# A DRAM buffer of its own for the last piece of each group, and kk loads in two parts

## The chip, the cores and the metric

The kernel runs on one core of one Trainium2 chip. The metric is device time in microseconds, from one launch. Three runs of the kernel before are shown, and one further execution was recorded by the hardware profiler; all rows below come from that one.

## The reference

Three stages, all in float32, chained. Only the first matters for the change.

```python
# q, k, v, a_re, a_im: (batch 4, heads 8, steps 768, 48)
scale = np.minimum(mag, 0.999) / (mag + 1e-06)          # mag = |a|
a_re_n, a_im_n = (a_re * scale, a_im * scale)
for t in range(S):
    new_re = ar * S_re - ai * S_im
    new_im = ar * S_im + ai * S_re
    S_re, S_im = (new_re + k[t] outer v[t], new_im)      # state 48 x 48 per head
    y[:, :, t] = q[t] @ S_re
# then, on x = y as (3072, 384):
#   mixture of 8 experts, one expert per row: gate * (relu(x @ w1[e]) @ w2[e])
#   out = ((x @ w1) * (x @ w2)) @ w3 @ w_out
```

## The kernel before, in words

**The work of the first stage.** The 768 steps are cut into three *groups* (NG = 3) of 256, a group into four chunks of 64 steps (C = 64). Within a chunk the recurrence is rewritten as products: with P(t) the running product of the complex factors a, the kernel forms q(t) P(t) and k(t) divided by P(t), so that a chunk is an ordinary masked attention of 64 steps plus the state handed over from the chunk before.

**Pieces, the elementwise stream.** `elementwise` (line 722) works with 128 lanes; a lane is one (pair of batches q, chunk c, head h, batch b of the pair), so lanes 0 to 63 are q = 0 and lanes 64 to 127 are q = 1. It runs over 24 *pieces* of 8 steps (TP = 8), eight to a group (NPC = 8). For each piece it loads a (line 710, two pieces in one load) and the raw q and k (line 719), makes the scaled factors on ScalarE and VectorE, the running product step by step on VectorE (lines 780 and 782), and with line 812 the tile `qk` of that piece: 8 steps, two kinds (q P and k / P), 96 numbers. Some of its additions run on TensorE as matmuls with the identity (line 736). The piece is then stored to the DRAM tensor `qkd` (line 607), whose order is group, q, c, head, b, step, kind, 96. The seven first pieces of a group are stored by one DMA from GpSimd's queue (line 820); the last one is split, lanes 0 to 63 by SyncE (line 817) and lanes 64 to 127 by GpSimd (line 818).

**Tiles, the second stream.** `groups` (line 1026) takes the eight (q, c) *tiles* of each group in turn. For a tile, `loads` (line 898) issues on SyncE two loads of v into the buffer `vz` (line 907, six slots) and one load of `kk` (line 909, four buffers, 768 KB): 128 partitions (b, step), in each 8 heads x 2 kinds x 96 numbers. So the DRAM tensor does the transposition from lanes to steps. `turn` (line 885) transposes kk on TensorE (line 893) and copies the result to SBUF on ScalarE (line 894); then follow the scores (line 921), the state chain (lines 978, 985, 992 to 994), the outputs (lines 940, 941) and the routing to experts (lines 109 to 163). At the start of a group, `ends` (line 867) prepares the group's last factors; in the first two groups it also issues eight dense matmuls on the last stored piece (`dense`, line 879).

**What orders the work.** Both streams are generators that `drive` interleaves by costs written in the code, so that the first tile loads of a group are written behind the store of its eighth piece (line 1051 waits for `made` to reach the end of the group, line 1054 issues the loads of the group's first two tiles; those of later tiles are issued at line 1069, after a tile's chain). That gives every instruction its place in the program. The Tile framework then sorts the instructions of each engine's queue by this order and by a simulated time at which they become ready, adds the waits, and an engine executes its queue strictly in order; a load may so be issued long before its place in the program. Dependencies through DRAM are tracked by address ranges. In a lane of `qkd` the eight pieces lie behind one another, so the range of any tile's first seven pieces also spans parts of its eighth.

In the third group VectorE, ScalarE and SyncE also convert weights for the last stage (class `Fuse`; lines 282 to 297), which use SyncE's queue for the `fdr` loads. After the groups follow the experts (`moe`) and the last stage (`moe2`), both almost all TensorE matmuls.

Of the kernel before, what the change touches and what calls it, by code (L numbers as in the profile page):

```python
# [8 lines left out]
F32 = mybir.dt.float32  # L9
# [86 lines left out]
def bc(ap, n, at):  # L96
    shape = list(ap.shape)
    return ap.unsqueeze(at).to_broadcast(shape[:at] + [n] + shape[at:])
# [463 lines left out]
NH = 8  # L562
SEQ = 768
D = 48
C = 64
NG = 3
TP = 8
NPC = C // TP
NPIECE = NG * NPC
R2 = 2 * D  # L570
# [16 lines left out]
def attn_consts(tc, S):  # L587
    nc = tc.nc
    c = S.cpool
    S.mask = c.tile([128, C], F32, tag="mask", name="mask")  # L590
    nc.gpsimd.memset(S.mask, 1.0)
    for h in range(2):
        m = S.mask[h * C : (h + 1) * C, :]
        nc.gpsimd.affine_select(out=m, in_=m, compare_op=ALU.is_ge, fill=0.0, base=0, pattern=[[1, C]], channel_multiplier=-1)
    S.perm = c.tile([R2, R2], F32, tag="perm", name="perm")
    nc.gpsimd.memset(S.perm, 0.0)
    nc.gpsimd.affine_select(out=S.perm, in_=S.perm, compare_op=ALU.not_equal, fill=1.0, base=D, pattern=[[1, R2]], channel_multiplier=-1)
    nc.gpsimd.affine_select(out=S.perm, in_=S.perm, compare_op=ALU.not_equal, fill=-1.0, base=-D, pattern=[[1, R2]], channel_multiplier=-1)
    S.wb = c.tile([128, 1], F32, tag="wb", name="wb")
    nc.gpsimd.memset(S.wb, 0.4995)  # L600
    S.tiny = c.tile([128, 2], F32, tag="tiny", name="tiny")
    nc.gpsimd.memset(S.tiny[:, 0:1], 2.0 ** -60)
    nc.gpsimd.memset(S.tiny[:, 1:2], 2.0 ** -100)
    S.sy = c.tile([128, NPIECE], F32, tag="sy", name="sy")
    S.su = c.tile([128, NPIECE], F32, tag="su", name="su")
    S.xm = c.tile([128, NG, D], F32, tag="xm", name="xm")
    S.qkd = S.dpool.tile([NG, 2, 4, NH, 2, C, 2, R2], F32, tag="qkd", name="qkd")


class Fuse:  # L610
# [85 lines left out]
class Attn:  # L696
# [25 lines left out]
    def elementwise(self, aside, factors):  # L722

        nc, S, ep, e2 = self.nc, self.S, self.ep, self.e2
# [74 lines left out]
        def keys(i):  # L799
            g, p = divmod(i, NPC)  # L800
            k = raw[i][:, :, 1]
            x, g0 = s2[i][:, 0], s2[i][:, 1]
            if p == NPC - 1:
                v.tensor_copy(S.xm[:, g], px[i][:, E - D :])
            v.tensor_tensor(out=x, in0=px[i], in1=g0, op=ALU.mult)
            yield 470
            v.tensor_tensor(out=k, in0=k, in1=td(g0), op=ALU.mult)
            yield 470
            v.scalar_tensor_tensor(out=k, in0=td(x), scalar=2.0, in1=k, op0=ALU.subtract, op1=ALU.mult, reverse0=True)
            yield 470  # L810
            self.qk[i] = o = self.qp.tile([128, TP, 2, 2, D], F32, tag="qk", name=f"qk{i}")
            S.end = v.tensor_tensor(out=o, in0=bc(P[i], 2, 2), in1=bc(raw[i], 2, 3), op=ALU.mult)
            yield 1740
            dst = S.qkd[g].rearrange("q c h b (p t) w e -> p (q c h b) (t w e)", p=NPC)[p]
            self.stored = self.qk.pop(i).rearrange("p t w r d -> p (t w r d)")
            if p == NPC - 1:
                nc.sync.dma_start(dst[:64], self.stored[:64])
                done = nc.gpsimd.dma_start(dst[64:], self.stored[64:])
            else:
                done = nc.gpsimd.dma_start(dst, self.stored)  # L820
            with self.tc.issue_after(done.ins):
                aside(i)
            self.made = i + 1
# [21 lines left out]
        for i in range(NPIECE + 1):  # L845
            if i:
                power(i - 1)
                weigh(i - 1)
            if i % 2 and i + 3 < NPIECE:
                a[i + 3], a[i + 4] = self.load_a(i + 3)  # L850
            if i + AHEAD < NPIECE:
                root(i + AHEAD)
            if i + 1 < NPIECE:
                raw[i + 1] = self.load_qk(i + 1)
            ends = [j >= 0 and j % NPC == NPC - 1 for j in (i - 2, i - 1)]
            rest = [keys(i - 2)] if i > 1 and not ends[0] else []
            if i + 1 < NPIECE:
                rest.append(norm(i + 1))
            if ends[1]:
                rest.append(keys(i - 1))  # L860
            if i + 2 < NPIECE:
                rest.append(excess(i + 2))
            yield from mix(*([prefix(i)] if i < NPIECE else []), chain(*rest))
            if i == NPIECE - 1:
                factors()
# [30 lines left out]
        self.qkT[u] = qkT  # L896

    def loads(self, u):
        nc, S, st = self.nc, self.S, self.st
        g, q, c = u  # L900
        t0 = (g * 4 + c) * C
        n = self.nv
        self.nv = (n + 1) % VBUF
        assert n not in self.held.values()
        self.held[u] = n
        for i in range(2):
            nc.sync.dma_start(self.vz[i * C : (i + 1) * C, n, i], S.v[2 * q + i, t0 : t0 + C, :])
        kk = st.tile([128, NH, 2, R2], F32, tag="kk", name="kk%d%d%d" % u, bufs=4)
        nc.sync.dma_start(kk, S.qkd[g, q, c].rearrange("h b t w e -> (b t) h w e"))
        return self.vz[:, n].rearrange("t i (h e) -> t i h e", e=D), kk  # L910

    def scores(self, u, qk):
# [113 lines left out]
    def groups(self, route, side, free):  # L1026

        nc, S, st = self.nc, self.S, self.st
        self.ca, self.cb, self.cc, self.at, self.qkT, self.xs = {}, {}, {}, {}, {}, []
        self.route = route  # L1030
        self.nv = self.slot = 0
        self.held = {}
        self.pool, self.turns = [], 0
        self.spare = None
        self.vz = st.tile([128, VBUF, 2, HD], F32, tag="vz", name="vz")
        nc.gpsimd.memset(self.vz, 0.0)
        for q in range(2):
            self.ca[q] = st.tile([R2, 2, HD], F32, tag=f"ca{q}", name=f"ca{q}")
            self.cc[q] = st.tile([R2, 2, HD], F32, tag=f"cc{q}", name=f"cc{q}")
            nc.gpsimd.memset(self.ca[q], 0.0)  # L1040
        yield lambda: self.made >= NPC
        self.W = self.pp.tile([128, 2, 512], F32, tag="W", name="W")
        work = [(g, q, c) for g in range(NG) for q in range(2) for c in range(4)]
        ld = {}
        step = 0
        for n, u in enumerate(work):
            g, q, c = u
            if q == 0 and c == 0:
                while self.pool and self.made < (g + 1) * NPC:
                    yield self.fill(1)  # L1050
                yield lambda: self.made >= (g + 1) * NPC
                yield from self.ends(g)
                for x in work[n : n + 2]:
                    ld[x] = self.loads(x)
                if g == NG - 1:
                    yield free
                    singles, spare = side.fuse.units, side.product
                    side()
            self.pool.append(Item("scores", self.scores(u, ld[u][1])))
            for x in self.chain(u, ld.pop(u)):  # L1060
                yield x
                yield self.fill(S.fillcost)
                step += 1
                if g == NG - 1:
                    for _ in range(1 + (step % 3 == 0)):
                        next(singles, None)
            for x in work[n + 1 : n + 3]:
                if x[0] == g and x not in ld:
                    ld[x] = self.loads(x)
        self.spare = spare  # L1070
        while self.pool:
            yield self.fill(1)
# [146 lines left out]
def build(ctx, tc, S):  # L1219
# [4 lines left out]
    nc.scalar.preload_act_table_set("natural_log_exp_and_others")  # L1224
    make_consts(tc, S)
    attn_consts(tc, S)
    S.xbufs, S.fillcost = XB, FILL
    with ExitStack() as at:
# [99 lines left out]
```

## Time and profile before

| | us |
|---|---|
| median of 3 runs | 1030.84 (1028.14 to 1032.24) |
| profiled execution, its own time | 1032.15 |
| span of that execution, first to last instruction | 1030.5 |
| TensorE (PE) busy in the span | 904.5 (88%) |
| VectorE (DVE) busy | 635.0 (62%) |
| ScalarE (ACT) busy | 486.8 (47%) |

The profile names engines PE (TensorE matmul), PEld (its weight load), DVE, ACT, POOL (GpSimd) and SP (SyncE; SPq is its DMA queue). All times in its rows count from the span's start. The groups' eighth pieces are stored at about 108, 220 and 313 us; the second stream of the first stage ends at about 414 us. "idle before <- X" is the time an engine stood still and what ended it.

### The profile page before, as it was taken

Reading aid. Unit: us, or ns where it says so; the run is one execution under the profiler, and the core shown is the slowest. Engines: PE = TensorE matmul, PEld = TensorE weight load, DVE = VectorE, ACT = ScalarE, POOL = GpSimd, SP = SyncE. Lnnn points to the kernel's source line nnn. Section 1 sums busy time; section 2 is a strip of 40 time slices with the busy share of each in tenths; the row PEclk is TensorE's granted clock in tenths of the full one; section 3 lists DMA queues with packets and bytes.
Section 4 is the critical chain, followed back from the end, with each engine's and each line's share of the span. In section 5 each row is a group of like instructions: output and inputs, shape, how many; then the busy total and the mean of one; then the engine's idle time right before and its main releaser. Section 6 shows DMA issues by size and latency. Waiting matters only on the chain. (4 is left out here: it accounts for less than half of the span.)

```text
span 1030.5 us, 17151 instructions
## 1 busy us (share of the span) xinstructions
PE 904.5 (88%) x6402; PEld 768.3 (75%) x6402; DVE 635.0 (62%) x1398; ACT 486.8 (47%) x1089; POOL 124.4 (12%) x196
## 2 busy tenths in 40 slices
PE   3435899968987999879999899999999999999991
PEld 1212478737866778879999789997888888888881
DVE  6899899988986778878999555543132323232220
ACT  6445688848864655435666444443121312121220
POOL 5111000220011001000122120110010101010101
PEclk8666899989987989999999999999999999999996
DMA  5556975459548633646676564530000000000001
GB/s 184 174 175 224 311 250 169 141 161 321 165 152 257 185 120 114 214 159 193 192 199 175 138 159 108 108 57 0 1 31 1 31 1 31 1 31 1 31 1 35
DMA packets 90190, 128.82 MB, mean 125 GB/s; under 512 B 7232, under 2 KB 72688, under 8 KB 90096
## 3 DMA queue, kind: packets, MB, share of 16 engines
q1 hardware_dynamic: 79408, 87.26, 29.4%
q0 software_dynamic: 10688, 40.36, 11.1%
q8 instruction: 53, 0.87, 0.4%
q14 instruction: 41, 0.34, 0.1%
HBM read 92.38 MB, written 35.22 MB: 124 GB/s over the span
## 5 line engine op out<-in xcount | busy, mean ns | idle before, releaser
L547 DVE TENSOR_TENSOR ab<-asb,pb 128x512 f32<-128x512 f32 x48 | 33.0, 688 | 189.6 <-PE pb L303 183.6
L297 DVE TENSOR_TENSOR l<-w,h 128x384 fp32r<-128x384 f32 x128 | 70.7, 556 | 50.3 <-ACT h L296 47.1
L296 ACT CAST h<-w 128x384 fp32r<-128x384 f32 x128 | 65.2, 513 | 76.8 <-PE ph L302 39.2
L542 ACT COPY asb<-pa 128x512 f32<-128x512 f32 x48 | 28.1, 586 | 123.4 <-PE pa L303 123.4
L736 PE MATMUL x<-s,ident 128*128 128x384 f32 x64 | 35.3, 691 | 50.9 <-ACT s L788 50.9
L296 ACT CAST gh<-ab 128x512 fp32r<-128x512 f32 x48 | 29.8, 621 | 94.3 <-DVE ab L547 94.3
L301 PE MATMUL py<-hh,h 128*128 128x432 f32 x192 | 69.5, 362 | 2.9 <-ACT hh L357 2.9
L302 PE MATMUL py<-hl,h 128*128 128x432 f32 x192 | 70.3, 366 | 1.1 <-DVE hl L358 1.1
L301 PE MATMUL ph<-xh,h 128*128 128x432 f32 x192 | 68.9, 361 | 1.0 <-DVE hl L358 1.0
L303 PE MATMUL ph<-xh,l 128*128 128x432 f32 x192 | 69.1, 360 | 0.0
L302 PE MATMUL ph<-xl,h 128*128 128x432 f32 x192 | 69.0, 359 | 0.0
L303 PE MATMUL py<-hh,l 128*128 128x432 f32 x192 | 68.9, 359 | 0.0
L780 DVE TENSOR_TENSOR pr<-cf,P 128x192 f32<-128x192 f32 x189 | 66.8, 354 | 3.2
L893 PE MATMUL tr<-ident,kk 128*96 128x128 f32 x384 | 58.7, 289 | 9.4 <-DMA kk<-qkd 8.0
L302 PE MATMUL po<-ol,gh 128*128 128x384 f32 x192 | 64.9, 338 | 0.0
L301 PE MATMUL po<-oh,gh 128*128 128x384 f32 x192 | 64.9, 338 | 0.0
L303 PE MATMUL po<-oh,gl 128*128 128x384 f32 x192 | 63.4, 338 | 0.0
L736 PEld LDWEIGHTS x<-s,ident 128*128 128x128 f32 x64 | 15.0, 257 | 64.5 <-ACT s L788 56.8
L894 ACT COPY qkT<-tr 96x512 f32<-96x512 f32 x96 | 53.7, 591 | 17.2 <-PE tr L893 16.8
L514 POOL DMA_INDIRECT out<-ob,mdp x24 | 23.8, 992 | 308.9 <-ACT ob L511 217.1
L301 PE MATMUL pa<-yh,ah 128*128 128x512 f32 x144 | 57.2, 397 | 2.0 <-ACT yh L296 2.0
L893 PEld LDWEIGHTS tr<-ident,kk 128*96 128x96 f32 x384 | 43.0, 133 | 19.7 <-DMA kk<-qkd 9.6
(221 smaller groups left out, 2438.4 us busy)
## 6 DMA issues: line engine op xcount, KB each, us to landing
w<-in_w SPq DMA_DIRECT2D x128, 192.0 KB, 3.2
kk<-qkd SPq DMA_DIRECT2D x24, 768.0 KB, 6.7
qkd<-qk POOLq DMA_DIRECT2D x21, 768.0 KB, 5.5
qkr<-in_qk SPq DMA_DIRECT2D x24, 384.0 KB, 3.8
a<-in_a SPq DMA_DIRECT2D x11, 768.0 KB
fdr<-in_w SPq DMA_DIRECT2D x16, 512.0 KB, 5.1
fdr<-in_v POOLq DMA_DIRECT2D x12, 512.0 KB, 4.8
xs<-zr POOLq DMA_DIRECT2D x8, 648.0 KB, 7.3
```

Source lines behind the costliest of these rows:

```text
L296: nc.scalar.copy(H, src)
L297: nc.vector.tensor_tensor(out=L, in0=src, in1=H.bitcast(F32), op=ALU.subtract)
L301: nc.tensor.matmul(out, lh, rh, start=first, stop=False)
L302: nc.tensor.matmul(out, lh, rl, start=False, stop=False)
L303: return nc.tensor.matmul(out, ll, rh, start=False, stop=last)
L514: nc.gpsimd.indirect_dma_start(out=out[j], out_offset=bass.IndirectOffsetOnAxis(ap=S.mdp[:, j, 0:1], axis=0), in_=ob, in_offset=None, boun ...
L542: nc.scalar.copy(asb, pa)
L547: nc.vector.tensor_tensor(out=ab, in0=asb, in1=pb, op=ALU.mult)
L736: nc.tensor.matmul(p, S.ident, s[r], start=r == 0, stop=r == 1)
L780: v.tensor_tensor(out=pr, in0=twice(cf[i][:, t]), in1=bc(pv, 2, 1), op=ALU.mult)
L893: nc.tensor.transpose(pt[:, h], qk[:, h0 + h, w], self.S.ident)
L894: nc.scalar.copy(qkT[:, w, h0 : h0 + 4], pt)
```

## The change

The DRAM tensor becomes two: one for the first 56 steps of each chunk (seven pieces), one for the last 8 (the eighth piece). `loads` is cut into `early` (the v loads and the first 56 steps of kk, one DMA for each b, 56 partitions) and `late` (the last 8 steps, one DMA for each b, 8 partitions). For the first two tiles of a group, `early` is written when seven pieces of the group are made, `late` when the eighth is; the other tiles call both, one behind the other. The second stream begins when seven pieces are made.

```diff
-    S.qkd = S.dpool.tile([NG, 2, 4, NH, 2, C, 2, R2], F32, tag="qkd", name="qkd")
+    S.qkd = [S.dpool.tile([NG, 2, 4, NH, 2, n, 2, R2], F32, tag=f"qkd{n}", name=f"qkd{n}") for n in (C - TP, TP)]
...
-            dst = S.qkd[g].rearrange("q c h b (p t) w e -> p (q c h b) (t w e)", p=NPC)[p]
+            dst = S.qkd[p == NPC - 1][g].rearrange("q c h b (p t) w e -> p (q c h b) (t w e)", t=TP)[p % (NPC - 1)]
...
     def loads(self, u):
+        x = self.early(u)
+        self.late(u, x)
+        return x
+
+    def late(self, u, x):
+
+        g, q, c = u
+        for b in range(2):
+            self.nc.sync.dma_start(x[1][(b + 1) * C - TP : (b + 1) * C], self.S.qkd[1][g, q, c, :, b].rearrange("h t w e -> t h w e"))
+
+    def early(self, u):
...
-        nc.sync.dma_start(kk, S.qkd[g, q, c].rearrange("h b t w e -> (b t) h w e"))
+        for b in range(2):
+            nc.sync.dma_start(kk[b * C : (b + 1) * C - TP], S.qkd[0][g, q, c, :, b].rearrange("h t w e -> t h w e"))
...
-        yield lambda: self.made >= NPC
+        yield lambda: self.made >= NPC - 1
...
             if q == 0 and c == 0:
+                while self.pool and self.made < (g + 1) * NPC - 1:
+                    yield self.fill(1)
+                yield lambda: self.made >= (g + 1) * NPC - 1
+                for x in work[n : n + 2]:
+                    ld[x] = self.early(x)
                 while self.pool and self.made < (g + 1) * NPC:
                     yield self.fill(1)
                 yield lambda: self.made >= (g + 1) * NPC
+                for x in work[n : n + 2]:
+                    self.late(x, ld[x])
                 yield from self.ends(g)
-                for x in work[n : n + 2]:
-                    ld[x] = self.loads(x)
```

## Rows read from the trace of the kernel before

**Rows 1.** Table of stretches: us, busy us (instructions) per engine, PEclk, DMA share, GB/s.
```profile
210.00:220.00 10.00, 2.36 (x11) 2.08 (x10) 8.48 (x26) 7.73 (x19) 0.00 (x0) 0.74 0.01 2
...
232.00:312.00 80.00, 73.33 (x1116) 62.13 (x1115) 71.85 (x177) 60.17 (x160) 7.35 (x10) 0.96 0.60 205
...
319.00:325.00 6.00, 0.41 (x3) 0.30 (x4) 2.93 (x9) 0.00 (x0) 3.01 (x3) 0.50 0.91 268
325.00:412.00 87.00, 83.38 (x1063) 69.86 (x1063) 66.99 (x145) 52.44 (x132) 7.22 (x7) 0.89 0.51 166
...
412.00:1030.00 618.00, 580.72 (x2941) 525.41 (x2937) 282.74 (x533) 219.58 (x429) 66.00 (x71) 0.98 0.29 79
```

**Rows 2.** TensorE's waits, windows 95:125, 205:235, 300:330: total us, times, longest.
```profile
PE tr L893 <- DMA kk<-qkd: 0.7, 1, 0.7
...
PE tr L893 <- DMA kk<-qkd: 1.7, 1, 1.7
...
PE tr L893 <- DMA kk<-qkd: 5.6, 1, 5.6
```

**Rows 3.** Timeline at the third group's start: start us, us, engine, line, what [idle before].
```profile
312.81 2.00 SPq L817 DMA_DIRECT2D qkd<-qk  x1
...
317.73 1.43 PE L149 MATMUL rk<-oh,ones 128*128 128x24 f32 x6
...
318.12 6.59 SPq L909 DMA_DIRECT2D kk<-qkd  x4
...
324.75 1.94 PE L893 MATMUL tr<-ident,kk 128*96 128x128 f32 x8 [5.59 <-DMA kk<-qkd]
...
329.04 1.90 PE L893 MATMUL tr<-ident,kk 128*96 128x128 f32 x8
```

**Rows 4.** Waits of ScalarE and VectorE, 312 to 330.
```profile
ACT qkT L894 <- PE tr L893: 7.0, 1, 7.0
...
DVE wol L297 <- ACT woh L296: 4.9, 1, 4.9
```

**Rows 5.** Timeline at the second group's start.
```profile
221.08 8.54 PE L883 MATMUL dense<-qk,ident 128*128 128x512 f32 x15
...
224.28 7.52 SPq L909 DMA_DIRECT2D kk<-qkd  x4
...
231.34 1.08 PE L893 MATMUL tr<-ident,kk 128*96 128x128 f32 x8 [1.72 <-DMA kk<-qkd]
...
233.53 0.56 DVE L805 TENSOR_TENSOR s<-s 128x384 f32<-128x384 f32 x1 [2.09 <-ACT s L797]
```

**Rows 6.** Timeline at the first group's start.
```profile
112.17 7.76 SPq L909 DMA_DIRECT2D kk<-qkd  x4
...
117.92 1.45 PE L736 MATMUL u<-sq,ident 128*128 128x384 f32 x4
```

**Rows 7.** Timeline of GpSimd's queue: stores of the seventh piece, second and third group.
```profile
201.39 0.58 POOL L820 DMA_DIRECT2D qkd<-qk  x1 [6.46 <-DVE P L782]
...
301.36 0.58 POOL L820 DMA_DIRECT2D qkd<-qk  x1 [5.36 <-DVE pr L780]
```

**Rows 8.** Issue (ns) and landing of kk, landing of vz and qkd, last store 200:236.
```profile
L909 SPq DMA_DIRECT2D kk<-qkd x24: 367/383/4247, 112.2 to 356.6; - x24
DMA to landing us min/median/max: 4.6/6.7/11.8
...
DMA to landing us min/median/max: 3.3/4.4/6.4
...
DMA to landing us min/median/max: 3.5/5.5/11.8
...
qkd<-qk SPq DMA_DIRECT2D x1, 384.0 KB, 4.1
```

**Rows 9.** Timeline: the a load before the second group's start and its reader.
```profile
205.14 0.63 SPq L710 DMA_DIRECT2D a<-in_a  x1
...
210.44 0.84 ACT L741 ACTIVATE sq<-a 128x768 f32<-128x768 f32 x1 [2.64 <-DMA a<-in_a]
```

## The prediction

> **What bounds the kernel now.** I read the table of stretches first, then the waits of TensorE at the three group starts, then the timeline around each start.
>
> In the table [rows 1] the last 618 us have TensorE busy for 580.72, so whatever starts that part earlier should end the kernel earlier. It is 83.38 of 87 us before that, in the tiles of the third group, and only 0.41 of 6 us in the stretch 319 to 325, where the third group starts. Before that start VectorE is the busiest of the engines that feed the third group (71.85 of 80 us): its piece-by-piece products decide when a group is complete. So two things count: holes in VectorE's work before 312 us, and the hole at the third group's start. What TensorE waits for in the first two groups costs something only if it reaches VectorE.
>
> TensorE waits for a kk load once in each group: 0.7, 1.7 and 5.6 us [rows 2]. In the third group [rows 3] the reader should see a chain: SyncE issues its half of the last piece's store at 312.81; the first kk load goes out at 318.12, when that store has landed; the first transposes start at 324.75, while TensorE's last earlier work ended at 317.73 + 1.43 = 319.16. The other engines stand with it: ScalarE waits 7.0 us for the transposes, and VectorE 4.9 us for a ScalarE cast queued behind that wait [rows 4]. In the second group [rows 5] the eight dense matmuls keep TensorE until 221.08 + 8.54 = 229.62, the transposes start at 231.34, and VectorE idles 2.09 us for a ScalarE step (L797) that stands behind the first copy of the transposes. In the first group [rows 6] TensorE's adds run to 117.92 + 1.45 = 119.37 and the transposes need kk only then; of the 0.7 us nothing reaches VectorE.
>
> **The change, part by part.**
>
> Two DRAM buffers in place of one: the stores stay as many and as large. Cost nothing; they are issued by the same engines.
>
> Each tile's single kk load becomes four: two of 56 steps, two of 8. That is 3 x 24 = 72 more issues on SyncE, at 0.38 us each [rows 8] 27.6 us of its queue in all. For a tile in the middle of a group this is 1.1 us more of a queue that is ahead of its use; what hides it is the four kk buffers. Without that cover it would be up to 1.1 us a tile. I cost it at nothing.
>
> The early loads now wait for the seventh piece's store, not the eighth's. That store leaves at 201.39 and 301.36 in the second and third group [rows 7] and takes 3.5 to 5.5 us to land [rows 8], so SyncE can send the early loads from about 205 to 207 and 305 to 307. In the old order four tiles' kk loads occupied SyncE for 7.76, 7.52 and 6.59 us [rows 3, 5, 6], because the last piece's landing frees all of them at once; I expect four tiles (two by the edit, the next two because only their buffers hold them) to move forward together, about 7 us of transfers. In the second group these fall on DMA engines that are idle (share 0.01 from 210 to 220 [rows 1]); in the third they end at 312 to 314, just when the last store is issued.
>
> After the last store has landed only the 8-step parts remain: two loads of 48 KB for the first tile. No row has such a load. The nearest is vz, 96 KB on 64 partitions, 3.3 us to landing at the least and 4.4 in the median [rows 8]; below stands zero, above the kk load's own 6.7. I take 3.3, because the load is half as large and the early loads are out of its way. The page "DMA: Bandwidth & Descriptors" of the Trainium skill (section "Anatomy of one DMA") gives about 2.0 us plus the bytes at 436 GB/s, an estimate of 2.1 us; by it the sum would be 1.2 us lower.
>
> Third group: 318.12 + 0.38 (the second issue) + 3.3 = 321.8 in place of 324.75, so **2.9 us** gained. Bounds: 1.8 with 4.4 us to landing, and 5.6 if the load is never waited for. What is late next is the second tile, whose transposes came at 329.04 [rows 3], 4.3 us after the first's; its two late loads follow 0.8 us behind, so it does not wait. The gain carries: ScalarE and VectorE are held by the same transposes and move with them, and the weight conversions they carry move too.
>
> Second group: 224.28 + 0.38 + 3.3 = 228.0, before the dense matmuls end at 229.62, so all of the **1.7 us** goes, and with it that much of VectorE's 2.09 us hole (the same time, counted once). Bounds: 0 if other ScalarE work fills the place, 2.1 if the whole hole closes.
>
> First group: the 0.7 us wait goes and I count **0**, as no VectorE wait hangs on it; bound 0.7.
>
> Added wait: SyncE runs in order, and its half of the last store (L817) now has early loads ahead of it. If one is being issued when the store is ready, that is **0.4 us** (one issue) in the third group, on the path. Bounds: 0, and about 2 us if the rings are still full at 312.8. In the first two groups the dense matmuls cover it. Behind the early loads' wait also stand loads of the next pieces (a, qkr): the slower rival below.
>
> Sum: -2.9 - 1.7 + 0.4 = -4.2 us. The profiled execution took 1032.15 us, so 1027.95; it lies 1.3 above the median of the runs shown (1030.84), and against that median the forecast is **1026.6 us**. A measurement of this kernel can tell about 0.5% (5.2 us) from no change, so the middle of this forecast is a gain just too small to tell.
>
> **Rivals.**
>
> *More than the sum.* All the waits go (5.6 + 2.1 + 0.7 = 8.4), and the loads of a and qkr, which now stand behind up to 7.8 us of kk issues at each group start, come earlier: 1022 less one or two more, 1020 to 1022. For it: VectorE and ScalarE stall together with TensorE in rows 4 and 5. Against: the late load cannot land at once. Chance 0.20.
>
> *Late loads stand in line.* The rings are still working on the early loads of the second pair of tiles when the late ones are issued, and these land hardly before 324.75. Only the second group's 1.7 us is left: 1029, with nothing left at all 1031. What speaks for it: from the last store on 64 partitions, 384 KB took 4.1 us, no less than a whole piece on 128 partitions at its best (3.5) [rows 8]; if loads on 56 partitions run at half the pace, the four tiles need some 14 us in place of 7, to about 320 us, and the late ones land near 323. The page "SBUF — State Buffer" of the Trainium skill (section "Door 1: The DMA port swizzle") has a rule against this change: partitions 0 to 63 reach only eight of the sixteen ports, and by its section "Can I just issue two DMAs to hit both halves?" a second transfer to the other half gains 6%. By that rule this rival's time is the one to expect. Against: that store of 384 KB was one of a pair in flight together, and 14 us still fit between the two stores of the second group. Chance 0.18.
>
> *Slower.* The order on SyncE decides. The a load that ScalarE waits for at 210.44 (2.64 us, already late) is issued at 205.14 [rows 9], within the time in which the early loads wait for the seventh store. If the early loads are put ahead of it, it goes out only after their wait and their issues: 206.9 + 7.5 = 214.4, 9.3 us later. VectorE has some other work there but idles already; the whole 9.3 less the 4.2 won is +5.1: 1036. If the same happens in the first group, whose engines are busier, up to 1042. It decides as soon as the early loads stand ahead of the a load in the queue; where they stand behind it, it costs nothing. For it: VectorE has little slack. Against: the a load is written earlier in the program than the early loads, so it has the older claim. A reordering of the other engines' instructions by the new readiness times can add a few us of either sign. Chance 0.16.
>
> *The change does not do what it says*: the early loads are not issued before the last store, for instance because kk buffers are not free. Four buffers for tiles, of which the third group's first two take those of tiles used long before 300 us, speak against it; it would give 1031, and I count it within the second rival.
>
> **How the numbers follow.** The forecast as worked out, 1023 to 1030, has 0.46. Faster by over 0.5% (below 1025.7) is the first rival and a third of the forecast's own chance: 0.20 + 0.16 = 0.36. Slower by over 0.5% (above 1036.0) is nearly all of the third rival, 0.14. The rest, 0.50, lies within. The range takes in the first rival to 1019 and the cheap half of the slower one, to 1036.
>
> **What would show it.** In the changed kernel's timeline: kk loads on SyncE before the store of L817 in each group, and two short ones after its landing; TensorE's wait for kk about 2.7 us in the third group and none in the second; VectorE's 2.09 us hole before L805 gone; the last piece's product (L812) of the third group ending about 1.7 us earlier. It is wrong if a loads are issued after the early kk loads and ScalarE's L741 waits longer than now, if the late load takes as long as the old kk load, or if the tiles after 325 us run at another pace than now.

## The result, and the profile after

The change made the kernel slower: **1045.0 us** (median of four runs, 1035.97 to 1054.47) against 1029.49 us before. The ratio is 1.0116 (95% interval 1.008 to 1.0152); it leaves out the longest run, which was in a slower state than the other three. The forecast was 1026.6 us, with 1036 as the upper end of its range.

The execution that the profiler recorded was that longest one (1054.47 us). Where a size matters, this section therefore also reads experiment e1 (next section), which runs the changed kernel's instructions in the same order on TensorE, VectorE and ScalarE, and whose profiled execution took 1041.49 us (span 1039.8).

The changed kernel's stretches: the third group's start, its tiles, and the rest. In the columns, TensorE's busy time comes first and its granted clock, the DMA engines' busy share and the traffic in GB/s stand last:

```profile
327.00:343.00 16.00, 11.34 (x206) 9.57 (x205) 10.97 (x22) 7.51 (x24) 0.59 (x1) 0.92 0.92 255
343.00:437.00 94.00, 91.71 (x1149) 76.41 (x1148) 72.59 (x167) 55.09 (x138) 11.01 (x10) 0.87 0.53 149
437.00:1052.00 615.00, 579.08 (x2879) 524.62 (x2877) 279.55 (x527) 219.40 (x427) 65.89 (x71) 0.98 0.29 79
```

The last two stretches of the kernel before, cut where the group's tiles end as above (at 414 us, 2 us later than in [rows 1]):

```profile
325.00:414.00 89.00, 85.38 (x1120) 71.80 (x1119) 68.92 (x149) 53.26 (x134) 7.22 (x7) 0.89 0.50 164
414.00:1030.00 616.00, 578.72 (x2879) 523.46 (x2878) 280.81 (x530) 218.76 (x427) 66.00 (x71) 0.98 0.29 79
```

The last stretch is what it was (579.08 us of TensorE in 615 against 578.72 in 616), so the loss arises before it, in the first stage. TensorE's hole at the third group's start is still there, 4.66 of the 16 us from 327 (11.34 busy), and the stretch behind it has grown from 89 to 94 us (in e1 to 92). TensorE's waits around the three group starts (95:140, 225:275, 310:350), which answer to [rows 2]:

```profile
PE tr L894 <- DMA kk<-qkd: 8.1, 1, 8.1
...
PE tr L894 <- DMA kk<-qkd: 3.6, 1, 3.6
...
PE tr L894 <- DMA kk<-qkd: 4.7, 1, 4.7
```

The waits that the change was to remove are together twice as long as before: 16.4 us in place of 8.0. In e1 they are 7.6, 3.7 and 4.1 us. Only the third group's became shorter, by 0.9 us. The worst is now the first group's start. Its timeline on SyncE, and below it GpSimd's half of the last store, the first transposes (TensorE) and the wait on VectorE behind them:

```profile
103.58 11.51 SPq L922 DMA_DIRECT2D kk<-qkd  x8
115.19 1.30 SPq L818 DMA_DIRECT2D qkd<-qk  x1
116.54 0.60 SPq L720 DMA_DIRECT2D qkr<-in_qk  x1
124.39 3.92 SPq L908 DMA_DIRECT2D kk<-qkd  x8
128.74 0.40 SPq L711 DMA_DIRECT2D a<-in_a  x1
...
107.77 0.56 POOL L819 DMA_DIRECT2D qkd<-qk  x1 [8.33 <-DVE P L783]
...
129.46 1.92 PE L894 MATMUL tr<-ident,kk 128*96 128x128 f32 x8 [8.11 <-DMA kk<-qkd]
...
131.59 0.56 DVE L806 TENSOR_TENSOR s<-x,s 128x384 f32<-128x384 f32 x1 [7.62 <-ACT s L798]
```

Read it from the top. The early loads go out where the change wants them, before the last store, and there are eight: four tiles, as the prediction expected. But they occupy SyncE for 11.51 us and not 7, so its half of the last store (L818) leaves at 115.19, though GpSimd's half left at 107.77. Once issued, that half takes 9.2 us until the first 8-step load can follow it (115.19 to 124.39); before, the same step took 4.2 us, from the store in the first line below to the first kk load at 112.17 [rows 6]. The same steps in the kernel before:

```profile
107.94 0.47 SPq L817 DMA_DIRECT2D qkd<-qk  x1
...
120.03 2.28 SPq L710 DMA_DIRECT2D a<-in_a  x1
...
120.10 1.08 PE L893 MATMUL tr<-ident,kk 128*96 128x128 f32 x8 [0.72 <-DMA kk<-qkd]
...
126.55 0.55 DVE L805 TENSOR_TENSOR s<-x,s 128x384 f32<-128x384 f32 x1
```

The a load that stands behind the kk loads went out at 120.03 before, and at 128.74 now. TensorE's adds end at 121.35 and the transposes start 8.11 us after them, and VectorE stands still for 7.62 us behind them: the place where the prediction had counted nothing.

Why eight loads take so long is seen in the traffic at moments when kk loads are nearly alone on the DMA engines: the changed kernel (107 to 108.2 us), e1 (107 to 108.6) and the kernel before (118 to 123), in this order:

```profile
DMA packets 312, 0.23 MB, mean 191 GB/s; under 512 B 13, under 2 KB 312, under 8 KB 312
...
DMA packets 458, 0.34 MB, mean 213 GB/s; under 512 B 14, under 2 KB 458, under 8 KB 458
...
DMA packets 2459, 1.86 MB, mean 372 GB/s; under 512 B 39, under 2 KB 2459, under 8 KB 2459
```

The 16 DMA engines are busy all the time in all three (the hardware queue alone has 0.98 of it or more). The 8-step loads are slower still: in e1 from 127 to 130 us, when almost nothing else moves, the traffic is 112 GB/s on the mean, and the engines are about half busy:

```profile
DMA  5555541002343543653223554456453594334459
...
DMA packets 486, 0.34 MB, mean 112 GB/s; under 512 B 55, under 2 KB 484, under 8 KB 486
```

How this carries on is seen in the start times of the pieces' product (L812, L813 after the change), the second piece of the second group and the last of the third group. Before, after, and e1 in this order:

```profile
129.91 1.75 DVE L812 TENSOR_TENSOR qk<-P,qkr 128x1536 f32<-128x1536 f32 x1
...
310.23 1.76 DVE L812 TENSOR_TENSOR qk<-P,qkr 128x1536 f32<-128x1536 f32 x1
```

```profile
135.34 1.74 DVE L813 TENSOR_TENSOR qk<-P,qkr 128x1536 f32<-128x1536 f32 x1
...
326.94 1.76 DVE L813 TENSOR_TENSOR qk<-P,qkr 128x1536 f32<-128x1536 f32 x1
```

```profile
135.73 1.75 DVE L812 TENSOR_TENSOR qk<-P,qkr 128x1536 f32<-128x1536 f32 x1
...
319.29 1.76 DVE L812 TENSOR_TENSOR qk<-P,qkr 128x1536 f32<-128x1536 f32 x1
```

E1 is 5.8 us behind at the first of these and 9.1 us at the last (319.29 - 310.23), and its span is 9.3 us longer than before (1039.8 - 1030.5). The stretch 120 to 163 of the first group's tiles, before and then in e1 (TensorE, its loads, VectorE, ScalarE, GpSimd; then granted clock, DMA share, GB/s):

```profile
120.00:163.00 43.00, 42.73 (x551) 33.99 (x552) 41.14 (x92) 37.63 (x101) 2.16 (x4) 1.00 0.83 279
```

```profile
120.00:163.00 43.00, 34.26 (x395) 26.59 (x396) 32.51 (x73) 27.79 (x72) 1.62 (x3) 0.88 0.73 215
```

Before, three engines are nearly full here, so nothing that is lost can be caught up; in e1 TensorE, VectorE and ScalarE each do 8 to 10 us less. So in e1 the loss is made around the first group's start, and at the last piece it is neither won back nor doubled; in between the distance swings, because e1's engines have another order of instructions than those of before. The changed kernel's own profile shows the same first step (5.4 us) and further losses after it, to 16.7 us at the last piece; this one execution alone shows those, and they stay unexplained.

One more line of the page gives the price over the whole execution, the hardware queue's share of the DMA engines' time, before and after, for the same bytes:

```profile
q1 hardware_dynamic: 79408, 87.26, 29.4%
```

```profile
q1 hardware_dynamic: 80080, 87.26, 31.2%
```

29.4% of 1030.5 us is 303 us; 31.2% of 1052.8 us is 328 us. The same 87.26 MB took 25 us more of all sixteen engines' time, about 1 us for each of the 24 tiles. Most of it is the kk loads' own: read from the trace packet by packet, their 24,576 packets of 768 bytes took 59.0 us of the sixteen engines before (38 ns each) and 79.8 us after (52 ns).

### The profile page after: what moved, and what is told of

It is laid out like the page before. It is cut to its first block, busy times and chain, and to the rows that moved or that the text cites. A ratio compares the mean times of both kernels' runs of the same rounds, so it can differ in the third digit from the quotient of the medians.

```text
span 1052.8 us, 17253 instructions
## 1 busy us (share of the span) xinstructions
PE 918.2 (87%) x6402; PEld 777.2 (74%) x6402; DVE 635.6 (60%) x1398; ACT 488.5 (46%) x1089; POOL 125.2 (12%) x196
## 3 DMA queue, kind: packets, MB, share of 16 engines
q1 hardware_dynamic: 80080, 87.26, 31.2%
## 5 line engine op out<-in xcount | busy, mean ns | idle before, releaser
L737 PE MATMUL x<-s,ident 128*128 128x384 f32 x64 | 37.9, 735 | 49.6 <-ACT s L789 48.8
L894 PE MATMUL tr<-ident,kk 128*96 128x128 f32 x384 | 62.4, 300 | 19.6 <-DMA kk<-qkd 16.4
```

The source lines that it names most:

```text
L737: nc.tensor.matmul(p, S.ident, s[r], start=r == 0, stop=r == 1)
L894: nc.tensor.transpose(pt[:, h], qk[:, h0 + h, w], self.S.ident)
```

## The experiments

Three theories stood after the result. **Shape** (theory S in the expectations): a load whose rows lie in one half of the 128 partitions (56 or 64 of them) moves at a lower rate, so that cutting kk by b makes its traffic take longer and delays everything that shares the DMA engines. **Queue** (theory Q): the early loads hold SyncE, and the last store and the a loads stand behind them. **Order** (theory R): the change gives the other engines' instructions another order, and that order costs the time. E2 to e5 were run first, then e1 and e6 to e8, then e9, e10 and e5 again. All ratios are against the kernel before on the same chip, with their 95% interval.

**e1: four loads, nothing else.** One DRAM buffer, the loads written in the old place; only the one kk load is cut in four.

```diff
-        nc.sync.dma_start(kk, S.qkd[g, q, c].rearrange("h b t w e -> (b t) h w e"))
+        kkd = S.qkd[g, q, c]
+        for lo, hi in ((0, C - TP), (C - TP, C)):
+            for b in range(2):
+                nc.sync.dma_start(kk[b * C + lo : b * C + hi], kkd[:, b, lo:hi].rearrange("h t w e -> t h w e"))
```

> The kernel before with its one DRAM buffer and the loads written where they were, but each kk load cut into four (56 and 8 steps, each half). Its instructions stand on TensorE, VectorE and ScalarE in exactly the changed kernel's order. If neither the second buffer nor the earlier place in the program does anything: ratio 1.006 to 1.017, as the changed kernel, with loads of 56 steps issued before the last store. If the buffer or the place matters: ratio below 1.004.

Measured: 1.0122 (1.0063 to 1.018), the whole of the change's loss. The order of instructions on TensorE, VectorE and ScalarE is exactly that of the changed kernel, and the 56-step loads move ahead of the last store by themselves (103.80 against 115.48 in the first group), so a range of 56 steps cut by b no longer counts as overlapping the last piece. The second DRAM buffer and the earlier place in the program do nothing here; the cut load is the change. Which of its consequences costs the time, e1 does not tell.

**e2: the last store whole on GpSimd's queue, in the changed kernel.** This takes the store out from behind the early loads.

```diff
-            if p == NPC - 1:
-                nc.sync.dma_start(dst[:64], self.stored[:64])
-                done = nc.gpsimd.dma_start(dst[64:], self.stored[64:])
-            else:
-                done = nc.gpsimd.dma_start(dst, self.stored)
+            done = nc.gpsimd.dma_start(dst, self.stored)
```

> The changed kernel, but the whole last store of a group goes out on GpSimd's queue, so that no store stands behind the early loads on SyncE. Theory Q (the order on SyncE: the half store is issued up to 7 us late behind eight early loads, and lands late behind them): most of the loss goes, ratio to the kernel before 0.995 to 1.004, the last store of the first group issued near 108 us in place of 115, first transposes near 121 in place of 129. Theory S (shape: loads on 56 partitions are slow wherever they stand): ratio stays at 1.008 or more. Theory R (new order of the other engines' instructions): ratio stays above 1.005 though the first transposes are early.

Measured: 1.0069 (1.0034 to 1.0105), between the ranges of Queue and Shape. The store left at once (GpSimd, 106.90), but the transposes of the first group still waited 8.7 us for kk. The reason is in the list of DMA issues of that moment (last number: us to landing):

```profile
qkd<-qk POOLq DMA_DIRECT2D x1, 768.0 KB, 10.2
```

Out of the queue, the store is late all the same: it shares the DMA engines with the early loads and lands after 10.2 us. So the queue is not the whole of it.

**e3: the store first, then the early loads** (only the first pair of tiles loads ahead of its own 8-step parts; the second pair follows them).

```diff
-                nc.sync.dma_start(dst[:64], self.stored[:64])
+                self.first = nc.sync.dma_start(dst[:64], self.stored[:64])
...
+        with self.tc.issue_after(self.first.ins):
+            for b in range(2):
+                nc.sync.dma_start(kk[b * C : (b + 1) * C - TP], S.qkd[0][g, q, c, :, b].rearrange("h t w e -> t h w e"))
...
```

> The changed kernel, but on SyncE the half store of the last piece goes first, then the first pair's 56-step loads, then their 8-step loads, then the second pair's. Theory Q: the loss goes and a part of the hoped-for gain comes, ratio 0.994 to 1.002; store at 108 us, first transposes of the groups at 117 to 121, 228 to 231, 320 to 324. Theory S: the two early loads take so long that the short ones land later than the old single load, ratio 1.005 to 1.015. Theory R: the starts are early but the ratio stays above 1.005.

Measured: 1.0254 (1.0188 to 1.0321), the slowest of all and above the range of every theory. The first group's store now leaves at 107.37, but SyncE's queue becomes longer behind it: the next a load goes out at 127.57 (before at 120.03), and its reader on ScalarE waits:

```profile
127.57 1.20 SPq L711 DMA_DIRECT2D a<-in_a  x1
...
138.76 0.84 ACT L742 ACTIVATE sq<-a 128x768 f32<-128x768 f32 x1 [5.76 <-DMA a<-in_a]
```

This is the slower rival of the prediction, an a load behind kk loads; since they are loads of 56 and 8 steps, their rate may have a part in it too.

**e4: the kernel before with the last store whole on GpSimd** (the edit of e2 on the kernel before), the control for e2.

> The kernel before with the whole last store of a group on GpSimd's queue: the control for the run above it. All theories: ratio 0.998 to 1.004; a whole piece lands up to 1 us later than two halves did.

Measured: **0.9916** (0.9882 to 0.995), faster than before, which no theory had expected. Against this control e2 is 1.5% slower: the store's place and the cut loads pull in opposite directions. The sizes are not clean, because e4's engines have another order of instructions than those of before and of e2; e7 and e8 below compare the store's place at one order.

**e5 and e5 again: the kernel before with two loads of 64 partitions**, one for each b. None can go ahead of the last store.

```diff
-        nc.sync.dma_start(kk, S.qkd[g, q, c].rearrange("h b t w e -> (b t) h w e"))
+        for b in range(2):
+            nc.sync.dma_start(kk[b * C : (b + 1) * C], S.qkd[g, q, c, :, b].rearrange("h t w e -> t h w e"))
```

> The kernel before, one DRAM buffer, with each kk load as two loads of 64 partitions that both need the last piece, so nothing can go early: shape alone. Theory S: ratio 1.006 or more, the first transposes 3 to 7 us later at each group start because half-partition loads move at half the pace. Theory Q: ratio 0.998 to 1.004, starts less than 2 us later. Theory R: anything from 0.995 to 1.01, with the starts unmoved.

> The kernel with two loads of 64 partitions for each kk (one for each b) again, on the same chip as e10_even_odd, since that kernel differs from it in nothing but the rows of each load. Theory and rival both: 1.010 to 1.023 of before as in its first run, packet time near 325 us.

Measured: 1.0164 (1.01 to 1.0228), and 1.0231 (1.0193 to 1.027) in its second run, beside e10. So a cut by b costs as much as the whole change or more, with nothing early in it. The time is what Shape expected, the path is not: in the first group the transposes start at 118.97, against 120.10 before, and not 3 to 7 us late. The loss comes through the a loads, as the next run shows.

**e10: the same two loads of 64 partitions, but the even and the odd steps.**

```diff
-        nc.sync.dma_start(kk, S.qkd[g, q, c].rearrange("h b t w e -> (b t) h w e"))
+        kkd = S.qkd[g, q, c].rearrange("h b t w e -> (b t) h w e")
+        for i in range(2):
+            nc.sync.dma_start(kk[i::2], kkd[i::2])
```

> The kernel before, every kk load cut into two of 64 partitions, but by even and odd steps, so that each load has rows in all parts of the 128 partitions. Number, size and place of the loads and the order of the instructions on every engine are those of e5_two_halves. Theory (a load whose rows lie in one half of the partitions moves at a lower rate): the hardware queue's packet time goes back from 31.0% of e5's span (325 us) to that of before, 29.4% of 1030 (303 us); in 120 to 130 us the traffic is near 393 GB/s and not 289; ScalarE's line 741 waits for its a load near 130 us at most 2 us in place of 6.0; time within 0.5% of before. Rival (two loads in place of one are what costs, by issue time, by the number of transfers in flight or by the order of instructions): as e5_two_halves, 1.012 to 1.02 of before, with packet time near 325 us.

Measured: 0.9987 (0.9964 to 1.0009), no difference from before. This is the deciding pair. E5 and e10 have the same number, size and place of loads, the same packets (79792), and the same order of instructions on every engine; only the rows in each load differ. The queue's line of e5 again, then of e10:

```profile
q1 hardware_dynamic: 79792, 87.26, 31.1%
```

```profile
q1 hardware_dynamic: 79792, 87.26, 29.2%
```

31.1% of 1049.9 is 327 us, 29.2% of 1027.9 is 300 us. The kk packets alone took 79.9 and 58.9 us of the sixteen engines. In 120 to 130 us, where the DMA engines are busy in both, the traffic in forty slices of 0.25 us (the first row is the busy share in tenths), of e5 again and then of e10:

```profile
DMA  9999999999999999999999999999999999999899
GB/s 230 215 270 366 375 270 215 237 350 375 326 215 227 320 428 341 224 233 289 366 369 320 218 215 270 203 209 341 316 409 335 406 479 393 381 430 479 332 418 467
```

```profile
DMA  9999999999999999999989999999999996899999
GB/s 378 366 375 363 381 366 372 372 372 375 366 381 369 396 403 439 430 418 442 393 344 356 393 381 442 455 492 430 393 442 418 381 363 273 298 344 378 366 375 363
```

The engines are fully busy in both, but with contiguous halves the rate falls again and again to about 215 GB/s, and with spread rows it stays near 370 and above; over these 10 us the mean is 322 against 386 (289 in the first run of e5). A view of busy shares alone would not show this; the GB/s row under it does. In e5 the a load leaves at 120.40, in e10 at 119.44, so the queue treats it alike; its reader on ScalarE waits 6.00 us in e5, and everything behind it waits too, while in e10 the same line starts at 127.78 without a wait. E5 again, ScalarE, TensorE, VectorE:

```profile
133.56 0.84 ACT L741 ACTIVATE sq<-a 128x768 f32<-128x768 f32 x1 [6.00 <-DMA a<-in_a]
...
135.23 1.59 PE L986 MATMUL W<-vz,kk 128*96 128x96 f32 x8 [5.10 <-ACT z L980]
...
137.07 0.56 DVE L757 SCALAR_TENSOR_TENSOR sq<-sq,y 128x384 f32<-128x384 f32 x1 [5.14 <-ACT y L755]
```

TensorE's granted clock is 0.929 on the mean of e5 again and 0.942 of e10; what part of the difference in time that makes, no run here separates.

**e6 and e9: four and two loads of 128 partitions, cut by head** (`kk[:, h : h + 2]` and `kk[:, h : h + 4]`).

> The kernel before, each kk load as four loads of all 128 partitions and two heads each; none can go early. Theory S (partitions: a load that spans only half of them moves its bytes at a lower rate): hardware queue's packet time stays near 29.4% of the span, ratio 0.996 to 1.006. Theory N (the number of loads on SyncE): ratio 1.010 or more, packet time near 31%. The order of the other engines differs here from every other kernel, so a ratio off by up to 0.008 for that alone is possible; the packet time is not touched by it.

> The kernel before, every kk load cut into two of 128 partitions and four heads. Here the order of the instructions differs from that of e5_two_halves. Theory: packet time as before, 303 us, traffic in 120 to 130 us near 390 GB/s; time within 0.7% of before, the rest being the order. Rival (two loads in place of one are what costs): 1.01 or more.

Measured: 1.007 (1.0045 to 1.0096) and 1.0079 (1.0046 to 1.0113). Their packet time is that of before (29.2% of 1033.8 and 29.0% of 1038.2, 302 and 301 us), so the number of loads adds no DMA time. They also read the DRAM tensor in the same runs of 64 steps as e5, so it is hardly the reading side that makes e5 slow. Some 0.7% is lost nevertheless. On every engine but GpSimd the order of the instructions differs much from that of before and of e5; that the order is what costs is likely but not shown. E6 missed its range (to 1.006) and e9 its bound of 0.7%, both by a little.

**e7: the four-way cut for the first two tiles of a group alone**; the others keep their one load. **e8** is e7 with the last store whole on GpSimd.

```diff
-        nc.sync.dma_start(kk, S.qkd[g, q, c].rearrange("h b t w e -> (b t) h w e"))
+        kkd = S.qkd[g, q, c]
+        if q == 0 and c < 2:
+            for lo, hi in ((0, C - TP), (C - TP, C)):
+                for b in range(2):
+                    nc.sync.dma_start(kk[b * C + lo : b * C + hi], kkd[:, b, lo:hi].rearrange("h t w e -> t h w e"))
+        else:
+            nc.sync.dma_start(kk, kkd.rearrange("h b t w e -> (b t) h w e"))
```

> One DRAM buffer, the kk load cut into four only for the first two tiles of each group, one load for the other six; half store on SyncE as before. TensorE and the other engines stand in the same order as with the whole store on GpSimd's queue (0.9916). Theory S: a quarter of the split loads, so a quarter of the extra packet time (29.9%); ratio 0.993 to 1.001. Theory Q: the half store still stands behind four early loads, starts of groups 2 to 4 us later than without, ratio 0.996 to 1.004. Theory R (the order makes the time): 0.990 to 0.993.

> As the run above it, with the whole last store on GpSimd's queue, so that no store stands behind the early loads. Same order of TensorE, VectorE and ScalarE as the whole store on GpSimd's queue alone (0.9916). If the early loads are worth what was hoped for once they are few and block no store: 0.986 to 0.990. If their cost in the DMA engines eats it: 0.991 to 0.996.

Measured: e7 1.0004 (0.9976 to 1.0033), e8 **0.9905** (0.9868 to 0.9943). Against e1, e7 takes away the cut of the 18 other tiles, and the whole loss is gone with it; but e7's engines have e4's order of instructions, not e1's, so a part of this may be the order's. And it is the change's idea at its purest: early loads where they are wanted and nowhere else. It gains nothing: e7 is level with before, and e8 with e4, which is the clean comparison, at almost the same order (0.9905 and 0.9916, the intervals overlap). TensorE's waits for kk are shorter (3.3 us in e7, 8.0 before), so where did that gain go? The last store of the third group, issued by GpSimd in both, in e4 and then in e8 (last number: us to landing):

```profile
qkd<-qk POOLq DMA_DIRECT2D x1, 768.0 KB, 3.7
```

```profile
qkd<-qk POOLq DMA_DIRECT2D x1, 768.0 KB, 8.0
```

With 56-step loads in flight the store lands 4.3 us later, and the 8-step loads wait for exactly that store. In the first group it is the same: from GpSimd's store to SyncE's first load behind it 9.0 us in e8 (108.86 to 117.87) and 5.45 in e4 (107.31 to 112.76). What the shorter last load saves, the later landing gives back. Late landings are not new with half loads, though: stores took up to 11.8 us in the kernel before [rows 8].

E7 and e8 have the same order on TensorE, and nearly so on VectorE and ScalarE; the 1% between them comes from the store's queue. The profile points to SyncE: in e7 an `fdr` load (weights) stands behind the wait for the last store and leaves at 320.80, in e8 ahead of it at 312.37. VectorE's conversion that reads it, in e7 and then in e8:

```profile
324.76 0.36 DVE L286 TENSOR_SCALAR fda<-fdr 128x384 int32<-128x384 int32 x1 [4.19 <-DMA fdr<-in_w_out]
```

```profile
318.91 0.36 DVE L286 TENSOR_SCALAR fda<-fdr 128x384 int32<-128x384 int32 x1 [0.23 <-DMA fdr<-in_w_out]
```

That this wait makes the 1% was not tried on its own.

## Why the prediction was wrong, point by point

*Two DRAM buffers cost nothing*: right, and more than that; e1 does without them and is the same program on the three computing engines.

*Four loads in place of one cost nothing for a tile in the middle of a group*: **this is the step that failed.** I priced the loads by their issues alone (1.1 us of SyncE for a tile, hidden by four kk buffers) and not by what they do to the DMA engines. Issues are indeed cheap: e10 has 24 more at no loss. But the cut by b puts each load into one half of the partitions, and its traffic then ran at 191 to 213 GB/s in place of 372 where kk loads had the engines almost to themselves; all kk packets together took 79.8 us of the engines in place of 59.0. The work behind which I had hidden the loads does not hide this, because the victims are other transfers: the a loads, the last store, the next tile's loads. E5 (1.6 and 2.3% lost) against e10 (nothing lost) shows the shape alone, at one order of instructions. In the changed kernel it takes another path than in e5, through the last store and kk itself, and how much the new order adds there is open: e1's order was not run with whole loads. With the cut only where the idea needs it (e7) the loss is gone.

*Four tiles' loads move forward together, about 7 us of transfers*: the number of tiles was right, the time was not: 11.51 us in the first group and 8.67 in the second. I took 7 us from loads of 128 partitions [rows 3, 5, 6], and the rows that spoke against it stood in the rivals and not in the sum.

*First group, 0 us*: it has the largest loss, a wait of 8.1 us on TensorE and 7.62 us on VectorE. I looked at what could be gained there and asked only whether the 0.7 us wait would go; the group's start, with the DMA engines busy for 0.83 of the time from 120 to 163 us, was the place with the least room for slower traffic.

*SyncE's half of the last store, +0.4 us behind one early issue*: the place was named and the size was wrong. In the first group SyncE's half left 7.4 us behind GpSimd's half (115.19 against 107.77). I said that the dense matmuls cover it in the first two groups; in the first they and the adds behind them end at 121.35, 8 us before kk is there.

*VectorE as the busiest engine before the third group's start*: in its own row [rows 1] TensorE, which adds for the pieces, is busy for longer, 73.33 against 71.85 of 80 us, so before that start TensorE had no more room than VectorE, and its waits in the first two groups were not free.

*Third group -2.9 us, second -1.7 us*: the third group's wait shrank by 0.9 us (5.6 to 4.7), the second's grew from 1.7 to 3.6. The first group's late load took 4.7 us, from the second issue at 124.39 + 0.38 to the transposes at 129.46, and not the 3.3 I took because "the early loads are out of its way". These were in the way of the store before it, and with the late load the next piece's 768 KB store was on the engines, issued at 123.54. The page "DMA: Bandwidth & Descriptors" of the Trainium skill (section "Anatomy of one DMA") gave an estimate of 2.1 us, for a DMA that GpSimd issues; this load, which SyncE issued, did not come near it.

*The rivals.* "Late loads stand in line" had the mechanism, half the pace on 56 partitions, and at 0.18 too small a chance; its price was the real error: I counted only the gain that would be lost (1029 to 1031 us), as if slower transfers could not make anything later than before. Had the 25 us that the cut adds to the DMA engines' time stood in the sum, beside 4.6 us of gains, its sign would have been open at the least. The page "SBUF — State Buffer" of the Trainium skill (section "Door 1: The DMA port swizzle") says that partitions 0 to 63 reach only eight of sixteen ports, and that what counts is which partitions a load reaches and not how many; the trace agrees, by e5 against e10 (at the same 64 partitions for each load, falls to about 215 GB/s against a steady 370). The slower rival named the right victim, ScalarE's wait for a, with a queue's order as its cause. E3 has that order and the wait (5.76 us); in e5 the wait is as long (6.00 us) with the a load at its old place in the queue, from the rate alone. *The change doesn't do what it says* did not happen: the early loads do leave before the last store.

*What would show it*: the kk loads before the store of L817 and short ones after its landing are there; the second group's vanished wait and the earlier last product are not. The hole before L805 shrank from 2.09 to 0.24 us, but VectorE stands for 4.79 us a little earlier, as the second group's tiles start:

```profile
262.02 0.56 DVE L733 TENSOR_TENSOR s<-s 128x384 f32<-128x384 f32 x1 [4.79 <-ACT s L789]
```

## What to carry to other kernels

A load cut in two for an earlier start has a price beside its issues: look at which partitions each part covers, and when a part lies in one half of them, charge the lower rate to every tile that is cut and to every transfer that shares the engines; cut only the loads that need it. When a load is moved ahead of the store that the rest waits for, ask first how long that store takes to land with this load in flight, because the gain can be handed back there. And a rival that says "less gain" should always be carried through to what becomes later than before.

## What was not expected of the hardware

Where the DMA engines are busy throughout, loads of 64 partitions fell again and again to about 215 GB/s when these were contiguous and stayed near 370 GB/s when they were every other one. A store of 768 KB that landed in 3.7 us with little beside it took 8.0 to 10.2 us with 56-step loads in flight. And a last store that is issued whole by GpSimd, where SyncE's and GpSimd's queues shared it before, came with a kernel about 0.9% faster (e4 0.9916; e8 0.9905 against e7 1.0004 at almost one order of instructions); only a part of the reason was read (the `fdr` wait above). E4 and e8 are both faster than the two kernels of this study, and their intervals overlap. Early loads with rows in both halves, which a cut by the last 8 steps of each b does not give, were not tried.
